# One row of wo loaded as two pieces, ahead of the third group, in a decode kernel with gated attention

## The chip, the cores and the metric

The kernel runs on one core of one Trainium2 chip. The metric is the time of one execution on the device in microseconds. Times of a kernel are given as the median of its runs. A profile is one such execution, taken by the hardware profiler; "span" is the time from its first to its last instruction, and times inside a profile count from the span's start.

## What is computed

One decode step for two sequences (B = 2, one new position each, D = 640), all in float32. Attention over a cache of 4096 positions with 32 heads of 128, a feed-forward layer with SiLU, and a gate that mixes the two:

```python
g = sigmoid((x * gate_w).sum(-1, keepdims=True))
q = (x @ wq).reshape(B, 1, 32, 128).transpose(0, 2, 1, 3)
p = softmax(einsum("bhqd,bhkd->bhqk", q, k_cache) * 128 ** -0.5)
o = einsum("bhqk,bhkd->bhqd", p, v_cache)
a = o.transpose(0, 2, 1, 3).reshape(B, 1, 4096) @ wo        # wo: 4096 x 640
b = silu(x @ w1) @ w2
return g * a + (1 - g) * b
```

The caches are by far the largest inputs; with the weights, 298 MB are read in one execution. wo is 10.5 MB of it.

## The kernel before

**Who orders the work.** The kernel first records operations, each with its engine, the names ("keys") that it reads and writes, and further operations that it comes after. Keys such as `b.3` stand for parts of a buffer. `Flow.plan` turns this into semaphore waits. Within an engine the order of recording is the order of execution, and an engine waits in place: what is queued behind a waiting operation waits too. A load is an operation of SP: SP waits for what the load depends on, issues it, and goes to the next. `f.users(keys)` gives the last writer of each key and its readers since then. An operation recorded `after` these waits for all of them, and where one of them is a load, for its landing.

**The attention.** The 32 heads of one sequence are taken four at a time (Q = 4), which makes 16 items (`items`, N = 16), ordered so that each of four groups n = 0..3 (NP = 4) has four items: two sets of four heads for each of two sequences. For an item, 8.4 MB of K and 8.4 MB of V are loaded, 64 KB to a partition. There are three such slabs in SBUF: K alternates between `a` and `b`, V goes to `v`; only the last item's V goes to `a`. In the loop over i, `products(i)` and `scores(i)` (VectorE and GpSimd) form the scores of item i, `weights(i)` the exponentials, while `values(i - 1)` multiplies V of the item before on TensorE (L799), `combine` and `gather` sum it up (L821, L837), and `turn` (L852 to L871) writes the result as columns into `oP`, the left operand of the last product. The keys of `oP` that it writes are `oP{n}{u}{b}`, one for each item, and `heads(g)` lists the four of group g.

**The output product.** wo has 4096 rows. Group g takes 1024 of them, eight for each partition (PR = 8): partition p holds rows 8p to 8p + 7 of the group side by side, 8 x 640 numbers. Groups 0, 1 and 2 lie in slab `v` after the last V there has been used, group 3 in slab `b` after the last K has been used (the last item is 15, and its K lies in `b`). `load_wo` issues them: groups 0 and 1 in one load, group 2 in one, group 3 in three cuts of 5, 2 and 1 rows (L325). Before the change all five loads are recorded together in the loop's round 15 (L909 to L912). "Row k" below is the k-th of the eight rows of every partition.

After the loop, `in_halves(g)` for g = 0, 1, 2 adds the groups' products into `early`, a PSUM tile of 128 x 320 that already holds the feed-forward's output (`ffn_out`): four strips of 32 partitions, two halves of the output's columns by two alternating places, and each strip's rows hold the two sequences 16 apart. Each row of a group is two matmuls, and each matmul in float32 shows as two instructions in the trace (L590: 64 for groups 0 and 1, 32 for group 2). `merge` copies `early` to SBUF on ScalarE (L602) and adds its strips into `acc` by a product with the matrix `join` (L607). `in_quarters(3)` then adds group 3 row by row to `acc`, four matmuls for each row (L620, eight instructions for each row, 64 in all), each row waiting for its cut. VectorE copies `acc` (L929) and SP sends out the result.

The left operand of a matmul is a window of 32 columns of `oP` (17 in `in_quarters`), which holds a group's row k for the two sequences 16 columns apart, with zeros elsewhere. `oP` has one place of 32 columns for each k and g, at LEAD + 32 * (k * NP + g), LEAD = 8.

**PSUM.** `ps_t` holds the sums of the exponentials (columns 0 and 1); `ps_acc` is `early`.

Of the kernel before, what the change touches and what calls it, by code (L numbers as in the profile page):

```python
# [189 lines left out]
def gated_decode(nc, x, kc, vc, wq, wo, w1, w2, gate, out):  # L190
    P = 128
    B, H, SK, DH = kc.shape
    D = x.shape[2]
# [13 lines left out]
    HB = 16  # L207
# [3 lines left out]
    W2 = D // 2  # L211
    NP = HQ // 2
    PR = 2 * Q
    FIRST = 5
    LEAD = HB // 2
    items = [(2 * n + u, b) for n in range(NP) for b in range(B) for u in range(2)]
    N = len(items)
    LOOPED = N - 1
# [2 lines left out]
    f = Flow(nc)  # L221
    V, S_, T_, G_ = nc.vector, nc.scalar, nc.tensor, nc.gpsimd
# [10 lines left out]
    slab = {n: slabs[:, k * SLAB : (k + 1) * SLAB] for k, n in enumerate("vba")}  # L233

    def part(n, *ks):
        return [f"{n}.{k}" for k in (ks or range(8))]

    ident = sb("ident", [P, P])
# [46 lines left out]
    PD = PR * D  # L285


    partial = slab["v"][:, (NP - 1) * PD :][:, :W2]
    ot = slab["v"][:, (NP - 1) * PD + W2 :][:, :W]

    def kslab(i):
# [22 lines left out]
    def load_wo(g):  # L314

        n, at = ("v", g * PD) if g < NP - 1 else ("b", 0)
        if g == 0:
            src = wo[: 2 * PR * P, :].rearrange("(g p n) d -> p g (n d)", g=2, n=PR)
            to = slab["v"][:, : 2 * PD].rearrange("p (g c) -> p g c", g=2)
            f.dma("SP", to, src, writes=part("v", 0, 1), after=v_users)  # L320
            return
        if g == 1:
            return
        src = wo[g * PR * P : (g + 1) * PR * P, :].rearrange("(p n) d -> p (n d)", n=PR)
        cuts = (0, PD) if g < NP - 1 else (0, FIRST * D, PD - D, PD)  # L325
        after = f.users(part(n)) if g == NP - 1 else v_users
        for k, (c0, c1) in enumerate(zip(cuts, cuts[1:])):
            f.dma("SP", slab[n][:, at + c0 : at + c1], src[:, c0:c1], writes=part(n, g % (NP - 1) + k), after=after)

    f.op("POOL", lambda: G_.memset(oP_xs, 0.0), writes=["oP", "xs"])
    f.dma("SP", slab["a"][:, : J * F], w1.rearrange("(p j) f -> p (j f)", j=J), writes=part("a"))
# [244 lines left out]
    def heads(g):  # L578
        return [f"oP{g}{u}{b}" for u in range(2) for b in range(B)]
# [32 lines left out]
        f.op("PE", fn, reads=["partial", "join"], writes=["ps_0"])  # L612

    def in_quarters(g):
        for k in range(PR):
            at = LEAD + 32 * (k * NP + g)

            def fn(k=k, at=at):
                for n in range(G):
                    last = T_.matmul(  # L620
                        acc[32 * n : 32 * n + HB + 1, :],
                        oP[:, at : at + HB + 1],
                        slab["b"][:, k * D + n * W : k * D + (n + 1) * W],
                        start=False,
                        stop=(k == PR - 1),
                    )
                return last

            f.op("PE", fn, reads=part("b", (k >= FIRST) + (k == PR - 1)) + heads(g), writes=["ps_0"])

    ffn_out("v")

# [69 lines left out]
    def products(i):  # L702
        k = slab[kslab(i)].rearrange("p (c d) -> p c d", d=DH)
        k0, k1 = part(kslab(i), 0), part(kslab(i), 1)
        f.op(
            "POOL",
            lambda: G_.tensor_mul(k[:, CV:, :], k[:, CV:, :], qsb[:, None, :].to_broadcast([P, C - CV, DH])),  # L707
            reads=["qsb"] + k1,
            writes=k1,
        )  # L710
        f.op(
            "DVE",
            lambda: V.tensor_mul(k[:, :CV, :], k[:, :CV, :], ps_q[:, None, :DH].to_broadcast([P, CV, DH])),  # L713
            reads=["ps_q"] + k0,
            writes=k0,
        )
# [170 lines left out]
    for i in range(N + 1):  # L887
        j = i - 1
        loop = j if 0 <= j < LOOPED else None

        def by(what):
            return [ops[what, j]] if loop is not None else ()

        steps.append(len(f.ops["DVE"]))
        turns.append(len(f.ops["ACT"]))
        if i < N:
            products(i)
        if j >= 0:
            values(j, by=[v_load[j]] if loop is not None else (), loop=loop)
            invert(j)  # L900
        if 1 <= i < N:
            load_v(i)
        if i < N:
            scores(i)
            if i + 2 < N:
                load_k(i + 2)
            peak(i)
            weights(i)
        if i == N - 1:  # L909
            v_users = f.users(part("v"))  # L910
            for g_ in range(NP):
                load_wo(g_)  # L912
        if j >= 0:
            combine(j)
            gather(j, by=by("combine"), loop=loop)
            turn(j)
        if i < N:
            inner = i if i < LOOPED else None
            total(i, by=[ops["exp", i]] if i < LOOPED else (), loop=inner)
            if i + 1 < N:  # L920
                query(i + 1, by=[ops["exp", i]], loop=inner)
                copy_q(i + 1)
    edges = steps[2 : N + 1 : 2]
    f.alike["DVE"] = [[f.ops["DVE"][a:b] for a, b in zip(edges, edges[1:])]]
    for g_ in range(NP - 1):
        in_halves(g_)
    merge()
    in_quarters(NP - 1)
# [60 lines left out]
```

## Time and profile before

| | |
|---|---|
| median of 3 runs | 695.91 us (695.84 to 696.04) |
| the profiled execution | 695.97 us |
| its span | 694.6 us |
| mean granted clock of TensorE | 0.661 of full speed |
| busy share of the span: DVE, POOL, PE, ACT | 73%, 38%, 31%, 6% |
| HBM read | 298.26 MB, 429 GB/s over the span |

The page has six parts: busy time of each engine; the span in 40 slices; DMA queues; the chain of work that ended last; the costliest groups of instructions; DMA issues. PE is TensorE's matmuls, PEld its weight loads, DVE VectorE, ACT ScalarE, POOL GpSimd, SP the engine that issues loads. L590 is line 590 of the kernel. A group's row gives the line, engine and operation, output and input, how often, and in brackets the time that the engine was idle just before and what ended it. In a table of stretches each row gives the busy time of PE, PEld, DVE, ACT and POOL with the number of instructions, then the granted clock of TensorE as a share of full speed, the mean busy share of the 16 DMA engines, and what they moved in GB/s. Packets are put down to the stretch in which they start, so shares over 1 occur in short stretches.

### The profile page before, as it was taken

How to read it: one execution, taken by the hardware profiler on the slowest of the kernel's cores; microseconds unless marked ns; L12 is line 12 of the kernel's file. 1: busy time of each engine (PE TensorE's matmuls, PEld its weight loads, DVE VectorE, ACT ScalarE, POOL GpSimd, SP SyncE). 2: the span in 40 equal slices, each digit the busy share in tenths (PEclk: the TensorE clock that was granted, in tenths of full speed). 3: DMA queues.
4: the chain of work that ended last, by engine and by line, in shares of the span. 5: the costliest groups of instructions: out<-in, count | busy, mean ns of one | idle time of the engine just before them, and what ended most of it. 6: DMA issues, size and time to landing. Idle time of an engine off the chain costs nothing. (4 is left out here: it accounts for less than half of the span.)

```text
span 694.6 us, 3767 instructions
## 1 busy us (share of the span) xinstructions
PE 211.9 (31%) x1440; PEld 70.2 (10%) x1440; DVE 506.9 (73%) x269; ACT 40.0 (6%) x152; POOL 265.6 (38%) x26
## 2 busy tenths in 40 slices
PE   0073033151331506060412305060513215060556
PEld 0031010010110101010100101010101001010112
DVE  3910958898989697886959596986959595977901
ACT  0001010101010101010010101010000101010100
POOL 1000908190827090815335180906244270907100
PEclk9997556565565657566575757575665757575779
DMA  9999999999999999999999999999999999999997
GB/s 383 429 426 473 426 423 427 423 464 434 423 430 423 442 457 423 423 430 434 464 423 423 430 426 468 426 423 430 423 468 430 423 430 423 453 445 423 430 417 309
DMA packets 6051, 298.32 MB, mean 429 GB/s; under 512 B 652, under 2 KB 672, under 8 KB 928
## 3 DMA queue, kind: packets, MB, share of 16 engines
q1 hardware_dynamic: 6048, 298.27, 99.3%
q8 instruction: 3, 0.05, 0.0%
HBM read 298.26 MB, written 0.01 MB: 429 GB/s over the span
## 5 line engine op out<-in xcount | busy, mean ns | idle before, releaser
L707 POOL TENSOR_TENSOR slabs<-slabs,qsb 128x7680 f32<-128x7680 f32 x16 | 262.4, 16400 | 378.9 <-DMA slabs<-in_A_k_cache_dram 330.8
L723 DVE TENSOR_REDUCE s<-slabs 128x68 f32<-128x8704 f32 (+1 forms) x32 | 276.3, 8677 | 0.0
L799 PE MATMUL ps<-slabs,pz 128*32 128x512 f32 x1024 | 147.2, 739 | 337.1 <-PEq L156 328.9
L713 DVE TENSOR_TENSOR slabs<-slabs,ps 128x8704 f32<-128x8704 f32 x16 | 147.5, 9221 | 103.8 <-DMA slabs<-in_A_k_cache_dram 103.2
L799 PEld LDWEIGHTS ps<-slabs,pz 128*32 128x32 f32 x1024 | 39.7, 132 | 433.5 <-issue 425.2
L752 ACT ACTIVATE pz<-s,nb 32x128 f32<-32x128 f32 x64 | 25.5, 398 | 545.8 <-PE ps L799 353.2
L837 PE MATMUL ps<-osb,pick 128*128 128x512 f32 x32 | 21.1, 747 | 60.9 <-PEq L156 59.9
L821 DVE SCALAR_TENSOR_TENSOR osb<-ps,rg,own 128x512 f32<-128x512 f32 x16 | 12.0, 750 | 23.4 <-PE ps L799 23.1
L852 DVE TENSOR_REDUCE row<-ps 64x128 f32<-64x512 f32 x16 | 10.9, 682 | 24.0 <-PE ps L837 24.0
L773 PE MATMUL ps<-rs,fold 128*128 128x1 f32 x32 | 6.2, 262 | 40.9 <-PEq L156 40.8
L475 DVE SCALAR_TENSOR_TENSOR slabs<-slabs 128x1728 f32<-128x1728 f32 x8 | 16.2, 2019 | 0.3
L487 PE MATMUL ps<-slabs,xz_col 128*32 128x432 f32 x16 | 3.1, 927 | 33.4 <-DVE slabs L475 33.4
L837 PEld LDWEIGHTS ps<-osb,pick 128*128 128x128 f32 x32 | 5.4, 211 | 75.0 <-issue 73.1
L752 ACT ACTIVATION_READ_ACCUMULATOR pz<-s,nb 32x1 f32 x64 | 11.8, 184 | 0.0
L773 PEld LDWEIGHTS ps<-rs,fold 128*128 128x128 f32 x32 | 6.2, 226 | 54.2 <-issue 53.3
L859 DVE STREAM_TRANSPOSE ps<-row 64x256 f32<-64x256 f32 x16 | 10.3, 643 | 0.6
L567 PE MATMUL ps<-slabs,seq 128*32 128x320 f32 x54 | 9.2, 496 | 3.7 <-DVE seq L546 3.7
L642 PE MATMUL ps<-slabs,xz_col 128*32 128x512 f32 x80 | 9.8, 593 | 0.0
L652 PE MATMUL ps<-qall,spread 128*128 (+1 forms) x32 | 9.0, 371 | 0.8 <-ACT qall L680 0.8
L929 DVE COPY slabs<-ps 128x160 f32<-128x160 f32 x1 | 0.3, 324 | 11.9 <-PE ps L620 11.9
L590 PE MATMUL ps<-slabs,oP_xs 128*32 128x320 f32 x96 | 6.9, 434 | 2.4 <-DMA slabs<-in_A_wo_dram 2.4
L652 PEld LDWEIGHTS ps<-qall,spread 128*128 128x128 f32 x32 | 6.1, 236 | 1.7 <-ACT qall L680 1.7
(63 smaller groups left out, 69.8 us busy)
## 6 DMA issues: line engine op xcount, KB each, us to landing
slabs<-in_A_wq_dram SPq DMA_DIRECT2D x1, 10240.0 KB, 44.5
slabs<-in_B_w_dram SPq DMA_DIRECT2D x2, 4320.0 KB, 16.9
slabs<-in_A_wo_dram SPq DMA_DIRECT2D x1, 5120.0 KB, 22.7
slabs<-in_A_wo_dram SPq DMA_DIRECT2D x1, 2560.0 KB, 28.3
slabs<-in_A_wo_dram SPq DMA_DIRECT2D x1, 1600.0 KB, 31.9
slabs<-in_A_wo_dram SPq DMA_DIRECT2D x1, 640.0 KB, 32.9
slabs<-in_A_wo_dram SPq DMA_DIRECT2D x1, 320.0 KB, 33.2
slabs<-in_A_k_cache_dram SPq DMA_DIRECT2D x16, 47.9
```

Source lines behind the costliest of these rows:

```text
L475: lambda b=b, j=j, at=at: V.scalar_tensor_tensor(hsum[:, b, :], w1t[:, j, :], at, hsum[:, b, :], op0=ALU.mult, op1=ALU.add)
L652: return T_.matmul(ps_q[:, :DH], spread, qall.rearrange("p n b u d -> p (n b u) d")[:, i, :], start=True, stop=True,)
L707: lambda: G_.tensor_mul(k[:, CV:, :], k[:, CV:, :], qsb[:, None, :].to_broadcast([P, C - CV, DH])),
L713: lambda: V.tensor_mul(k[:, :CV, :], k[:, :CV, :], ps_q[:, None, :DH].to_broadcast([P, CV, DH])),
L723: lambda c0=c0, c1=c1: V.reduce_sum(Ss[i % 2][:, c0:c1], k[:, c0:c1, :], axis=AX.X),
L752: last = S_.activation(pz[lo:hi, :, 4 * q : 4 * q + 4], s[lo:hi].rearrange("p (g c) -> p g c", c=4), AF.Exp, bias=nb[lo:hi], scale=SCALE, ...
L773: lambda *_: T_.matmul(ps_t[:, :1], fold.rearrange("p a q c -> p (a q c)"), rs, start=True, stop=True),
L799: last = T_.matmul(ps_v[32 * q : 32 * q + 32, :], pz[:, gr, :], v[:, gr, :], start=(gr < 4), stop=(gr >= NG - 4),)
L821: lambda: V.scalar_tensor_tensor(osb, ps_v.rearrange("p (c d) -> p c d", d=DH), rg, own[:, :, None].to_broadcast([P, 4, DH]), op0=ALU.mult ...
L837: lambda *_: T_.matmul(ps_o, pick, osb.rearrange("p c d -> p (c d)"), start=True, stop=True),
L852: lambda: V.reduce_sum(row, ps_o[:64].rearrange("p (c d) -> p d c", d=DH), axis=AX.X),
L859: lambda: V.transpose(oT.rearrange("p n (e i) -> p n e i", e=2), twice),
```

## The change

Row 7, the last of group 3's eight, no longer comes as the last cut. It is loaded ahead of group 2, in two loads: partitions 0 to 87 to their own place in slab `b` (HELD = 88), and the 40 rows of partitions 88 to 127 onto the even partitions 0, 2, ... 78 of `moved`, another place in slab `b` (MOVED = 80 partitions). The rest of group 3 comes in cuts of 5, 1 and 1 rows.

For the 40 rows, the left operand must stand on the even partitions too. `shift` is a matrix of 128 x 80 whose even columns are the columns 88 to 127 of the identity; `set_apart` multiplies `oP`'s two columns of row 7 by it on TensorE into `ps_t` and VectorE copies them to `apart`, a window like those of `oP`. `shift`, `apart` and `moved` are cleared with `blank` by one memset. `add_spared` adds both pieces into `early`, two matmuls each, before group 2; `in_quarters` has seven rows left.

What is recorded moves as well. In round 15 only groups 0 and 1 are loaded. In the round after the last item, VectorE's memset of `blank` and the copy to `shift` come first, then the two new loads, group 2 and group 3. The new loads come after all users of slab `b`, the memset among them; `load_wo(3)` asks for the users of `b` again after the new loads have been recorded. `set_apart` is recorded ahead of all of `in_halves`.

```diff
+    HELD = 8 * 11
+    MOVED = 2 * (P - HELD)
...
+    blank = slab["b"][:, PD:][:, : D + MOVED + 2 * HB + LEAD]
+    moved, shift, apart = blank[:MOVED, :D], blank[:, D : D + MOVED], blank[:MOVED, D + MOVED :]
...
-        cuts = (0, PD) if g < NP - 1 else (0, FIRST * D, PD - D, PD)
+        cuts = (0, PD) if g < NP - 1 else (0, FIRST * D, PD - 2 * D, PD - D)
...
+    def load_spared():
+        rows = wo[(NP - 1) * PR * P :, :].rearrange("(p n) d -> p n d", n=PR)[:, PR - 1, :]
+        after = f.users(part("b"))
+        f.dma("SP", slab["b"][:HELD, PD - D : PD], rows[:HELD], writes=part("b", 3), after=after)
+        f.dma("SP", moved[::2], rows[HELD:], writes=part("b", 4), after=after)
...
     def in_quarters(g):
-        for k in range(PR):
+        for k in range(PR - 1):
...
-                        stop=(k == PR - 1),
+                        stop=(k == PR - 2),
...
-            f.op("PE", fn, reads=part("b", (k >= FIRST) + (k == PR - 1)) + heads(g), writes=["ps_0"])
+            f.op("PE", fn, reads=part("b", max(0, k - FIRST + 1)) + heads(g), writes=["ps_0"])
+
+    def set_apart(g):
+        at = LEAD + 32 * ((PR - 1) * NP + g)
+        f.op(
+            "PE",
+            lambda: T_.matmul(
+                ps_t[:MOVED, 4:6], shift, oP[:, at : at + HB + 1 : HB], start=True, stop=True
+            ),
+            reads=["shift"] + heads(g),
+            writes=["ps_t"],
+        )
+        f.op(
+            "DVE",
+            lambda: V.tensor_copy(apart[:, LEAD : LEAD + HB + 1 : HB], ps_t[:MOVED, 4:6]),
+            reads=["ps_t"],
+            writes=["apart"],
+        )
+
+    def add_spared(g):
+        own_row = oP[:HELD, 32 * ((PR - 1) * NP + g) :], slab["b"][:HELD, PD - D : PD]
+        for e, (a, w) in enumerate((own_row, (apart, moved))):
+
+            def fn(e=e, a=a, w=w):
+                for n in range(2):
+                    at = LEAD // 2 * n
+                    last = T_.matmul(
+                        early[64 * e + 32 * n :][:32, :],
+                        a[:, at : at + 32],
+                        w[:, n * W2 : (n + 1) * W2],
+                        start=False,
+                        stop=False,
+                    )
+                return last
+
+            f.op("PE", fn, reads=part("b", 3 + e) + ["apart"] + heads(g), writes=["ps_acc"])
...
         if i < N:
             products(i)
+        else:
+            f.op("DVE", lambda: V.memset(blank, 0.0), writes=part("b") + ["shift", "apart"])
+            f.op(
+                "DVE",
+                lambda: V.tensor_copy(shift[:, ::2], ident[:, HELD:]),
+                reads=["ident", "shift"],
+                writes=["shift"],
+            )
+            load_spared()
+            for g_ in range(NP - 2, NP):
+                load_wo(g_)
...
             v_users = f.users(part("v"))
-            for g_ in range(NP):
+            for g_ in range(NP - 2):
                 load_wo(g_)
...
+    set_apart(NP - 1)
     for g_ in range(NP - 1):
+        if g_ == NP - 2:
+            add_spared(NP - 1)
         in_halves(g_)
     merge()
     in_quarters(NP - 1)
```

## The prediction

> **What bounds the kernel now.** I read the page first. The columns of its DMA part are queue, packets, MB and share of 16 DMA engines.
>
> ```profile
> span 694.6 us, 3767 instructions
> DMA packets 6051, 298.32 MB, mean 429 GB/s; under 512 B 652, under 2 KB 672, under 8 KB 928
> q1 hardware_dynamic: 6048, 298.27, 99.3%
> q8 instruction: 3, 0.05, 0.0%
> ```
>
> The loads keep all 16 DMA engines busy for 99.3% of the span, and the change moves not one byte less. So it can act only on what follows the moment when the first DMA engine runs out of work. The chain of waits shows that end (start, us, what):
>
> ```profile
> 657.78 31.89 DMA slabs<-in_A_wo_dram
> ...
> 689.80 2.16 PE ps L620 x56
> ...
> 691.99 0.51 PE ps L620 x8
> ...
> 692.52 0.32 DVE slabs L929
> ```
>
> The last row of wo lands, eight matmul instructions (0.51 us) and one copy follow. Third view: the last microseconds cut into stretches; the last two columns are DMA share and GB/s.
>
> ```profile
> 690.10:690.30 0.20, 0.20 (x16) 0.20 (x8) 0.00 (x0) 0.00 (x0) 0.00 (x0) 1.00 0.29 115
> 690.30:690.50 0.20, 0.20 (x13) 0.19 (x9) 0.00 (x0) 0.00 (x0) 0.00 (x0) 1.00 0.19 77
> ...
> 691.10:691.30 0.20, 0.20 (x12) 0.07 (x8) 0.00 (x0) 0.00 (x0) 0.00 (x0) 1.00 0.19 77
> 691.30:691.50 0.20, 0.20 (x12) 0.18 (x12) 0.00 (x0) 0.00 (x0) 0.00 (x0) 1.00 0.13 51
> 691.50:691.70 0.20, 0.20 (x16) 0.12 (x4) 0.00 (x0) 0.00 (x0) 0.00 (x0) 1.00 0.00 0
> ```
>
> A share of 0.19 is 3 of 16: thirteen DMA engines are done by 690.3, and three work on to about 691.4. Nobody takes work from those three, so a load's rows are tied to their DMA engine. The kernel's time is that of the slowest three, some 1.2 us behind. Three is also the number of q8 packets, which are instruction code. The DMA view of 684 to 686 us shows one of them:
>
> ```profile
> q8 instruction: 1, 0.02, 3.0%
> ```
>
> 3.0% of 16 DMA engines over 2 us is 0.96 us on one DMA engine: a DMA engine that has fetched code stays that much late to the end. That the three late ones are the three that fetched is my reading of it.
>
> **The change part by part.** *Loads.* In the rows above three DMA engines move 77 GB/s, 25.7 each, so a piece of 2560 B (one partition's row) takes 0.100 us. Taking one row out of the last cuts takes 8 pieces, 0.80 us, from every DMA engine. The 88 partitions in place give 8 pieces back to eleven of them if they are spread eight to each as the 128 are; the 40 rows give 4 pieces to ten, if four to each. So five DMA engines end 0.80 us earlier, one ends as before, ten end 0.40 us later. If the three late ones are among the five, they end at 691.4 - 0.8 = 690.6, the ten at 690.2 + 0.4 = 690.6, and the last landing moves from 691.99 to 691.2. If one of them is among the ten, it moves to 692.4.
>
> The count of small packets bears on the spread: 652 packets under 512 B are 40 x 16 + 12, a completion for each DMA engine of the forty large loads and four for each of the small loads of x, gate and the output. A load of few rows therefore does run on fewer DMA engines. [...]
>
> *SP's queue.* The two new loads wait for the memset on VectorE, and loads 2 and 3 of wo stand behind them. Load 3 also waits until the two have landed, since their keys are among those it asks for.
>
> ```profile
> 0.83 0.17 DVE L359 MEMSET ones<- 128x128 f32 x1 [0.83 <-PEq L979]
> 4.75 0.09 DVE L423 MEMSET join<- 128x34 f32 x1
> 656.84 2.31 SPq L72 DMA_DIRECT2D slabs<-in_A_wo_dram  x5
> 660.65 0.22 DVE L871 SCALAR_TENSOR_TENSOR oP_xs<-ps,side,oE 64x8 f32 x1 [0.16 <-DVE oE L865]
> 676.81 0.75 DVE L821 SCALAR_TENSOR_TENSOR osb<-ps,rg,own 128x512 f32<-128x512 f32 x1 [15.59 <-PE ps L799]
> 692.88 0.60 SPq L72 DMA_DIRECT2D out_dram<-slabs  x1
> ```
>
> The memset of 128x760 is bounded by 0.17 us and, at the 0.08 us for 94 columns between its two rows, by about 0.75; I take 0.7. It and the small copy run after 660.9, in VectorE's 15.59 us of idling. The issues slip from 657 to 662; ahead of them in the queue lie the last V, needed until 667.5, and the first 5 MB of wo until 679.6, so the slip costs nothing. The two new loads land at 679.7 to 680.9 (1.2 us behind the first groups on the ten). SP then issues three loads at 2.31 / 5 = 0.46 us each. The 8 rows of load 2 keep even a relieved DMA engine busy for 6.3 us after the first groups, to about 684. That leaves over 2 us; without this cover, each microsecond late would be one at the end.
>
> *TensorE.* The tail rows:
>
> ```profile
> 667.50 9.16 PE L799 MATMUL ps<-slabs,pz 128*32 128x512 f32 x64 [8.15 <-DMA slabs<-in_A_v_cache_dram]
> 658.96 0.38 PE L773 MATMUL ps<-rs,fold 128*128 128x1 f32 x2
> 677.61 1.12 PE L837 MATMUL ps<-osb,pick 128*128 128x512 f32 x2 [0.95 <-DVE osb L821]
> 679.63 4.51 PE L590 MATMUL ps<-slabs,oP_xs 128*32 128x320 f32 x64 [0.89 <-DMA slabs<-in_A_wo_dram]
> 680.44 0.22 DVE L871 SCALAR_TENSOR_TENSOR oP_xs<-ps,side,oE 64x8 f32<-64x8 f32 x1
> 685.64 2.36 PE L590 MATMUL ps<-slabs,oP_xs 128*32 128x320 f32 x32 [1.50 <-DMA slabs<-in_A_wo_dram]
> 688.54 0.47 PE L607 MATMUL ps<-slabs,join 128*17 128x160 f32 x8 [0.55 <-ACT slabs L602]
> 689.77 1.25 PEld L620 LDWEIGHTS ps<-slabs,oP_xs 128*17 128x17 f32 x40 [1.10 <-issue]
> 689.80 2.65 PE L620 MATMUL ps<-slabs,oP_xs 128*17 128x160 f32 x64 [0.80 <-DMA slabs<-in_A_wo_dram]
> ```
>
> `set_apart` stands first in TensorE's queue and waits for the last `turn`, which ends at 680.44 + 0.22 = 680.66. Behind it are all 64 instructions of groups 0 and 1, which now start at 679.63. They will start at 680.9 (0.05 to be released, 0.2 for the two shift instructions, half of L773's 0.38). Less about 0.43 for the last one's drain, 64 take 4.08 us, 0.065 each, so they end at 685.0; the eight of `add_spared` at 0.065 end at 685.5. Group 2 lands at 685.64, no later than now on the ten (1.2 early, 1.2 more work). So at full clock this wait is hidden.
>
> But TensorE is now idle from 678.73 to 680.7, 2.0 us instead of 0.9, and the granted clock answers to that. The windows of 3.41 us are where the clock changes; the first busy column is PE, the third from the end is the clock:
>
> ```profile
> 57.40:60.81 3.41, 1.57 (x9) 0.41 (x3) 0.00 (x0) 2.28 (x4) 0.00 (x0) 0.99 0.75 327
> 152.96:156.37 3.41, 1.85 (x20) 0.35 (x12) 3.41 (x1) 0.00 (x0) 2.73 (x1) 1.00 1.29 557
> 658.14:661.55 3.41, 1.09 (x4) 0.30 (x2) 2.07 (x6) 0.76 (x4) 0.00 (x0) 0.99 1.33 577
> 661.55:664.96 3.41, 0.00 (x0) 0.00 (x0) 0.00 (x0) 0.00 (x0) 0.00 (x0) 0.50 0.80 346
> 668.38:671.79 3.41, 3.41 (x24) 0.79 (x20) 0.00 (x0) 0.00 (x0) 0.00 (x0) 0.51 1.03 444
> 678.62:682.03 3.41, 2.52 (x37) 1.20 (x40) 1.78 (x4) 0.00 (x0) 0.00 (x0) 1.00 0.98 420
> ```
>
> After 57.40 (1.57 us busy) and 658.14 (1.09) the clock is halved; after 152.96 (1.85) and 678.62 (2.52) it is kept. A window that holds the whole 2.0 us gap is busy 1.4 us at most: halved. If a boundary cuts the gap, both windows reach 1.75 (halfway) only with the boundary between about 679.06 and 679.44, counting the 0.95 idle ahead of L837: 0.4 of 3.41 us. So in nine placements of ten one window at half clock falls on groups 0 and 1, and half of the 2.2 to 3.4 us that lies on work is lost: 1.1 to 1.7 us; I take 1.5. Group 2 then starts at 685.5 + 1.5 = 687.0. From its start to the join's is 688.54 - 685.64 = 2.90 us as now; the join's 8 issues take 0.25 (1.25 / 40 = 0.031 each), the remaining 56 of L620 1.75, the last drain 0.26 (0.51 - 0.25): 5.16 in all. The last matmul ends at 692.16, against 692.50 now. The landing at 691.2 gives 691.7, which is earlier: **TensorE ends last, 0.34 us sooner than now**.
>
> [...]
>
> **The sum.** The profiled execution took 695.97 us, 1.37 beyond its span of 694.6, and 0.06 over the median of 695.91. 695.97 - 0.34 = 695.63; against the median 695.57. I say 695.6.
>
> **The rivals.** *The clock is kept.* Then the landing decides: -0.79, 695.1. For it: one placement in ten, and a `turn` that comes earlier when the half-clock part of L799 is shorter (667.50 starts at half clock, and where the window ends is chance), so that the gap's loss is absorbed by the wait for group 2. *A late DMA engine is among the ten* that get 12 pieces and give 8: the last landing is 0.40 later, and TensorE, even halved, is hidden behind it: 696.3. No view names DMA engines. The packet records, which no view prints singly, can be joined end to start: none of the three late ones seems to be one of the four that carried x and gate, and the three begin the first load later than those four. That speaks for the five, weakly. *Slower beyond doubt:* the two new loads spread over fewer DMA engines than I took, as the small ones over four do. Four would carry 22 + 10 = 32 pieces, 3.2 us, less the 0.8 taken off. A DMA engine that is not late has 1.2 us of room, so it decides from 20 pieces on, and here it is +1.2 us; if a late one is among the four, +2.4: 697.1 to 698.3. [...] That the change does nothing, its loads shared evenly after all, is 695.9 and inside the forecast's range.
>
> **How the numbers follow.** Relieved and halved 0.45 (695.3 to 696.1 with the 1.1 to 1.7 us and the shift of `turn`); relieved, clock kept or its loss absorbed 0.18; a late one among the ten 0.27; fewer DMA engines 0.06; anything else, such as a fourth code fetch, 0.04. The first three lie within 0.2% (1.4 us, about what a measurement can tell from no change), 0.90 together. No case gains 1.4 us, 0.02 is left for the unforeseen. Slower: 0.06 + 0.02 = 0.08. The range 695.0 to 696.5 holds the first three with the bounds of their terms.
>
> **What would show it.** In the changed profile: L590's group of 64 starting at 680.7 to 681 behind `set_apart`; a granted clock of 0.5 in some window from 679 to 686 and that group lasting 5.6 to 6.2 us; no idle time of PE before the eight last matmuls. With the clock at 1.0 throughout, PE waits for a wo load there instead. After about 690.6 the DMA share should fall at once rather than stand at 0.19; a stand at 0.06 to 0.19 until 691.8 means that late ones were loaded more. A DMA share well under 0.9 between 680 and 688 would mean that SP's hold on load 3 starved the queue, which I exclude.

## The result and the profile after

| | before | changed |
|---|---|---|
| median | 695.92 us | 697.41 us |
| lowest and highest of 22 runs each | 695.66 to 697.04 | 695.93 to 698.81 |
| profiled execution, its span | 695.97, 694.6 | 696.56, 695.2 |

The ratio is 1.0021, with a 95% interval of 1.0014 to 1.0027: the change costs 1.5 us, and its runs spread over 2.9 us where the kernel before spreads over 1.4. The profiled execution of the changed kernel, at 696.56, is the fifth lowest of its 22 runs; what it shows is less than what the median pays, and the experiments have to find the rest.

The page of the changed kernel:

```profile
span 695.2 us, 3777 instructions
...
DMA packets 6200, 298.32 MB, mean 429 GB/s; under 512 B 673, under 2 KB 693, under 8 KB 1077
...
q1 hardware_dynamic: 6197, 298.27, 99.3%
q8 instruction: 3, 0.05, 0.0%
```

673 packets under 512 B are 21 more than the 652 of before, 11 + 10: the two new loads run on eleven and ten DMA engines, as the prediction took it. The bytes are the same. The chain of waits of its last part (start, us, what):

```profile
681.29 9.57 DMA slabs<-in_A_wo_dram
690.87 0.04 issue
690.91 2.14 PE ps L629 x56
693.05 0.02 issue
693.07 0.33 DVE slabs L987
```

It now ends over the landing of the cut of five rows at 690.87, behind which all 56 instructions of the last part run in one go. Before, 56 of these started at 689.80 and only the last eight waited. The last row lands at 692.40 (before 691.99), just early enough not to be waited for. So every load of the end is late, not the last one alone. TensorE's timeline (start, us, in brackets the idle time ahead and what ended it):

```profile
678.45 1.12 PE L881 MATMUL ps<-osb,pick 128*128 128x512 f32 x2 [0.95 <-DVE osb L865]
681.53 0.30 PE L644 MATMUL ps<-oP_xs,slabs 128*80 128x2 f32 x2 [1.96 <-DVE oP_xs L915]
681.77 4.51 PE L599 MATMUL ps<-slabs,oP_xs 128*32 128x320 f32 x64
...
687.12 2.36 PE L599 MATMUL ps<-slabs,oP_xs 128*32 128x320 f32 x32 [0.30 <-DMA slabs<-in_A_wo_dram]
690.02 0.47 PE L616 MATMUL ps<-slabs,join 128*17 128x160 f32 x8 [0.55 <-ACT slabs L611]
690.91 2.10 PE L629 MATMUL ps<-slabs,oP_xs 128*17 128x160 f32 x56 [0.42 <-DMA slabs<-in_A_wo_dram]
```

Groups 0 and 1 wait for `set_apart` as forecast, but run at full clock (4.51 us). Group 2 starts 1.48 us later than before (687.12 against 685.64) and ended a wait for its load: TensorE is not what is late. The stretches of the end (last two columns: DMA share, GB/s):

```profile
690.40:690.80 0.40, 0.09 (x4) 0.00 (x0) 0.00 (x0) 0.00 (x0) 0.00 (x0) 1.00 0.92 365
690.80:691.20 0.40, 0.29 (x9) 0.25 (x13) 0.00 (x0) 0.00 (x0) 0.00 (x0) 1.00 0.79 314
691.20:691.60 0.40, 0.40 (x20) 0.35 (x12) 0.00 (x0) 0.00 (x0) 0.00 (x0) 1.00 0.46 179
691.60:692.00 0.40, 0.40 (x20) 0.35 (x12) 0.00 (x0) 0.00 (x0) 0.00 (x0) 1.00 0.12 45
```

In the forecast nearly all were to be done at 690.6. Here nearly all 16 are at work until 690.8 (share 0.92) and half of them until 691.6. The bytes of 690.4 to 691.6 were missing earlier. Wider stretches of both kernels show where: first before, then changed.

```profile
666.00:674.00 8.00, 6.50 (x44) 1.68 (x48) 0.00 (x0) 0.00 (x0) 0.00 (x0) 0.64 0.98 420
674.00:682.00 8.00, 6.16 (x66) 2.01 (x62) 2.53 (x5) 0.00 (x0) 0.00 (x0) 1.00 1.01 435
682.00:690.00 8.00, 5.16 (x80) 2.07 (x76) 0.00 (x0) 0.42 (x1) 0.00 (x0) 1.00 0.97 406
```

```profile
666.00:674.00 8.00, 6.49 (x36) 1.62 (x40) 0.00 (x0) 0.00 (x0) 0.00 (x0) 0.54 1.03 443
674.00:682.00 8.00, 5.08 (x44) 1.40 (x39) 2.64 (x6) 0.00 (x0) 0.00 (x0) 1.00 0.99 369
682.00:690.00 8.00, 7.18 (x104) 3.02 (x96) 0.03 (x1) 0.43 (x1) 0.00 (x0) 1.00 0.97 412
```

From 674 to 682, while the two new loads run (they land between 678.9 and 681.3), the DMA engines are as busy as before (share 0.99) and move 369 GB/s. Measured on 420, the rate that a row of all 128 partitions in one load will have there (below), 8 x (1 - 369/420) = 0.97 us of transfer are lost. A share near one with fewer bytes says that packets take longer, not that the queue was empty. The packet records agree: row 7's pieces of 2560 B take 102 to 312 ns here, half of them 134 or more, and 102 ns each in the kernel that loads the row in one load (`whole_row`, below).

### The profile page after: what moved, and what is told of

It is laid out like the page before. It is cut to its first block, busy times and chain, and to the rows that moved or that the text cites. A ratio compares the mean times of both kernels' runs of the same rounds, so it can differ in the third digit from the quotient of the medians.

```text
span 695.2 us, 3777 instructions
## 1 busy us (share of the span) xinstructions
PE 213.5 (31%) x1442; PEld 70.7 (10%) x1442; DVE 507.4 (73%) x272; ACT 40.0 (6%) x152; POOL 265.7 (38%) x26
## 5 line engine op out<-in xcount | busy, mean ns | idle before, releaser
L843 PE MATMUL ps<-slabs,pz 128*32 128x512 f32 x1024 | 148.5, 745 | 335.4 <-PEq L156 328.1
L843 PEld LDWEIGHTS ps<-slabs,pz 128*32 128x32 f32 x1024 | 40.2, 133 | 432.4 <-issue 425.0
```

The costliest lines, as they stand in the source:

```text
L843: last = T_.matmul(ps_v[32 * q : 32 * q + 32, :], pz[:, gr, :], v[:, gr, :], start=(gr < 4), stop=(gr >= NG - 4),)
```

## The experiments

Every kernel is the changed kernel with the edit shown, unless it says otherwise. The theories, with the letters that the expectations use: **P**, TensorE's wait for the last `turn` and the half clock behind it make the time; **D**, the slow transfers from 674 to 682 make it; S and U are two causes for that slowness: **S**, a row loaded in parts, each onto fewer than 128 partitions, holds all DMA engines back while its loads run (my guess at the reason, that several DMA engines then write to the same part of the partitions, is one that no run shows); **U**, DMA engines with unequal work run apart and lose by it; **L**, which DMA engines have fetched code, and so are late, differs from execution to execution, and the changed kernel gives most of them more to do; **F**, the opposite of L, that it is the same ones each time.

**The same kernel again.** No edit.

> The changed kernel as it is, for a second profile and its spread beside the other runs. In the first profile the packets of the two new loads and those of group 2 behind them took 1.5 times their usual time between 678.2 and 681 us (280 GB/s instead of 430), which costs about 1.0 us on every DMA engine. Theory D (transfers): this stretch of 3 us is there again and decides the median of about 697.4. Theory P (TensorE's wait for the last turn, with the clock halved in most runs): the slow stretch is chance; here the clock is at 0.5 in a window between 679 and 686 and the group of 64 at in_halves takes about 6 us instead of 4.5.

Median 697.44 (695.90 to 698.94; ten runs: four up to 696.28, six from 697.13), ratio 1.0023 [1.0012, 1.0033]. Its profiled execution took 695.90 and differs from the first in both causes under dispute. Its window of 3.41 us with the gap, and the next one (third column from the end: granted clock):

```profile
677.81:681.22 3.41, 1.45 (x16) 0.63 (x18) 1.92 (x5) 0.00 (x0) 0.00 (x0) 1.00 1.07 390
681.22:684.64 3.42, 3.42 (x32) 1.31 (x25) 0.00 (x0) 0.00 (x0) 0.00 (x0) 0.50 0.97 418
```

Its chain:

```profile
680.60 6.14 PE ps L599 x64
686.74 0.54 PE ps L664 x8
687.28 2.20 PE ps L599 x32
...
690.45 1.97 PE ps L629 x56
692.42 0.02 issue
692.44 0.33 DVE slabs L987
```

This is the forecast's likeliest case in kind: 1.45 us busy, clock halved, 64 instructions in 6.2 us, no wait for a load behind them, last matmul at 692.42 where 692.16 was forecast. And it is the lowest of its ten runs, 695.90. So the half clock is real, and by itself it doesn't make the median.

**The wait moved out of the way** (`late_apart`): `set_apart` stands behind groups 0 and 1, just ahead of `add_spared`.

```diff
-    set_apart(NP - 1)
     for g_ in range(NP - 1):
         if g_ == NP - 2:
+            set_apart(NP - 1)
             add_spared(NP - 1)
```

> set_apart is recorded just ahead of add_spared, so TensorE starts groups 0 and 1 when they land and not behind the last turn; the loads are as in the change. Theory P: the median falls by 1 us or more, to 696.4 or less, and the spread of 695.9 to 698.8 shrinks to some tenths. Theory D: the median stays within 0.3 us of the changed kernel's, about 697.2, and the spread stays.

697.02 (695.89 to 699.08), ratio 1.0017 [1.0007, 1.0028]. In its profile the group of 64 starts at 680.42, waiting for its load and not for `turn`, and takes 4.51 us; the median and the spread stay. P is out as the cause of the median.

```profile
680.42 4.51 PE L599 MATMUL ps<-slabs,oP_xs 128*32 128x320 f32 x64 [1.41 <-DMA slabs<-in_A_wo_dram]
```

**40 rows on their own partitions** (`split_in_place`): no even partitions, no shift, no `set_apart`; `add_spared` is one product over all 128.

```diff
         f.dma("SP", slab["b"][:HELD, PD - D : PD], rows[:HELD], writes=part("b", 3), after=after)
-        f.dma("SP", moved[::2], rows[HELD:], writes=part("b", 4), after=after)
+        f.dma("SP", slab["b"][HELD:, PD - D : PD], rows[HELD:], writes=part("b", 4), after=after)
```

> The 40 rows go to their own partitions 88 to 127 and not onto even ones, so shift, set_apart and the second operand are gone; the two loads keep their sizes and their spread over eleven and ten DMA engines, and TensorE does not wait for the last turn. Theory P: no wait, so 695.2 to 695.6. Theory D with the uneven spread as cause: slow stretch of about 3 us at 430 to 280 GB/s as in the change, 696.5 or more. Theory D with the even partitions as cause: no slow stretch, 695.2 to 695.6.

697.57 (696.20 to 698.44), ratio 1.0021 [1.0011, 1.0030]; 369 GB/s from 674 to 682, as in the changed kernel. Where the 40 rows land doesn't matter; that the row is split in two loads is left.

**The row in one load** (`whole_row`): as `split_in_place`, with one load of 128 partitions ahead of group 2.

```diff
-        f.dma("SP", slab["b"][:HELD, PD - D : PD], rows[:HELD], writes=part("b", 3), after=after)
-        f.dma("SP", moved[::2], rows[HELD:], writes=part("b", 4), after=after)
+        f.dma("SP", slab["b"][:, PD - D : PD], rows, writes=part("b", 3, 4), after=after)
```

> Row 7 goes in one load of 128 partitions, in place, ahead of group 2: the order of the change without its uneven spread, and without shift, set_apart and a wait of TensorE. Both theories: 695.9 within 0.3, as before the change, with 2560-byte packets at 102 ns. If the slow stretch is there too, neither the uneven spread nor the even partitions cause it, but rows of 2560 bytes ahead of rows of 20480 bytes, and the time is 696.5 or more.

696.00, nine runs of ten between 695.89 and 696.27 and one at 697.46; ratio 1.0003 [0.9993, 1.0013]. Its stretch:

```profile
674.00:682.00 8.00, 5.97 (x66) 2.06 (x62) 2.52 (x5) 0.00 (x0) 0.00 (x0) 1.00 0.98 420
```

Loss and spread are both gone. The order of the loads, the memset, and the slip of the queue are all still in this kernel: the whole cost lies in the split. It relieves nobody either, so it doesn't tell S, U and L apart.

**Two halves, equal work** (`halves`): `whole_row` as two loads of 64 partitions. Each load has 16 times 4 rows, so each DMA engine gets 8 pieces, as before.

```diff
-        f.dma("SP", slab["b"][:, PD - D : PD], rows, writes=part("b", 3, 4), after=after)
+        f.dma("SP", slab["b"][: P // 2, PD - D : PD], rows[: P // 2], writes=part("b", 3), after=after)
+        f.dma("SP", slab["b"][P // 2 :, PD - D : PD], rows[P // 2 :], writes=part("b", 4), after=after)
```

> As whole_row, but row 7 comes in two loads of 64 partitions, 0 to 63 and 64 to 127. If each of the 16 DMA engines takes four rows of each load, no DMA engine gets more than another, yet the first load writes to one half of the partitions alone. Theory U (the slow stretch comes from DMA engines running apart, some already in group 2 while others have the pieces): no slow stretch, 696.0 as whole_row. Theory S (it comes from several DMA engines writing to the same few partitions' side of SBUF at once, which holds all of them back): a slow stretch from about 678.3 on, 2560-byte packets at 150 to 210 ns instead of 102, and the time longer by 0.5 to 1.5 us, 696.5 to 697.5.

697.88 (697.47 to 699.08), ratio 1.0029 [1.0018, 1.0040]. The page counts 684 packets under 512 B, 652 + 32: both loads use all 16 DMA engines, and no one is relieved or loaded more. The stretch, and then the chain:

```profile
674.00:682.00 8.00, 5.41 (x51) 1.44 (x43) 2.52 (x5) 0.00 (x0) 0.00 (x0) 1.00 1.01 338
```

```profile
682.86 9.60 DMA slabs<-in_A_wo_dram
692.46 0.04 issue
692.50 2.14 PE ps L629 x56
```

8 x (1 - 338/420) = 1.56 us are lost, and the cut of five rows lands at 692.46, 1.6 us behind the changed kernel's. U cannot make this, since the work is equal; S can. From 679 to 680 the trace shows 182 GB/s, under half of the 429 that the kernel before has over its span. Why a load of 64 partitions holds the DMA engines back is not shown, for no view tells which DMA engine writes to which partitions; that the smaller loss with 88 and 40 rows, 0.97 us, has the same cause is inferred. The runs of `halves`, with equal work for all, still spread from 697.47 to 699.08, so unequal work isn't the only source of spread.

The loss differs between executions, and the last landing goes with it. Eight profiles with the row split 88 and 40, in the order of their rate from 674 to 682, with `whole_row` and `halves` as ends (GB/s, last landing, time of the profiled execution):

| kernel | GB/s | last landing | us |
|---|---|---|---|
| whole_row | 420 | 691.79 | 695.93 |
| after_again | 392 | 691.75 | 695.90 |
| after_p4 | 392 | 691.84 | 695.99 |
| after_p5 | 389 | 691.62 | 695.81 |
| late_apart | 387 | 691.82 | 696.02 |
| after_p3 | 376 | 692.38 | 696.56 |
| changed | 369 | 692.40 | 696.56 |
| split_in_place | 369 | 692.28 | 696.43 |
| after_p2 | 364 | 692.81 | 696.97 |
| halves | 338 | 694.00 | 698.14 |

Without the loss the split rows would end at the forecast's 691.2; 392 GB/s is a loss of 0.53 us, 369 of 0.97, 364 of 1.07. With these the sum gives 691.7, 692.2 and 692.3; measured are 691.8, 692.4 and 692.8.

**Four more profiles of the changed kernel** (`after_p2` to `after_p5`), for the table and for the clock.

> The changed kernel once more, for a profile of one of its slower executions. Both theories on the slow stretch: if the time is 697 us or more, the stretch below 350 GB/s lasts longer than the 3 us of the execution at 696.56 and the 2 us of that at 695.9, by about 1.5 us for each microsecond of time. If instead the stretch is as long and TensorE waits or runs at half clock, the spread is TensorE's.

> As after_p2, one more execution: the time against the length of the stretch below 350 GB/s, and the granted clock between 679 and 686 us.

> The changed kernel, for a profile of one of its slower executions. If it takes 698 us or more: theory P, a window at half clock lies on group 2 or on the last group (32 instructions taking 4 us and not 2.4, as in own_ports), while the last landing is at 692 to 693; theory S alone, the last landing is at 694 or later.

> The changed kernel once more, for a profile of one of its slower executions. If it takes 698 us or more: theory P, a window at half clock lies on group 2 or on the last group, while the last landing is at 692 to 693; theory S alone, the last landing is at 694 or later.

A window at half clock fell on groups 0 and 1 in `after_p2` and `after_p3` (6.21 and 6.17 us for the 64), not in `after_p4` and `after_p5` (4.51). Over all six profiles it is three of six, with 696.56, 695.99 and 695.81 at full clock and 695.90, 696.97 and 696.56 at half: no order by the clock. All six lie under 697.0, though, while 22 of the 30 runs of this kernel outside these profiles lie above it, up to 698.9. None reached the 697 or 698 us for which the expectations were written, so these profiles decide nothing about the slower executions. S as they show it makes 695.8 to 697.0 and no more; something that no profiled execution of the changed kernel shows is still missing.

**Uneven work by loads of 8 rows** (`own_ports`): `whole_row`, and ten more loads of 8 rows each onto partitions four apart, whose data nothing uses, though `add_spared` waits for their landing; eight DMA engines carry 10 pieces more, a packet each (that such loads run on eight fits the landings of `tail_load`, below).

```diff
+        for n in range(10):
+            lo = 32 * (n // 4 % 2) + n % 4
+            at = PD + 2 * D + D * (n // 8)
+            f.dma("SP", slab["b"][lo : lo + 29 : 4, at : at + D], rows[lo : lo + 29 : 4], writes=[f"extra{n}"], after=after)
```

> [...] Theory U: slow stretch, 2560-byte packets over 150 ns, 696.5 or more. Theory S: no slow stretch, packets at 102 ns, 696.0 to 696.3, since the ten packets end before the three late DMA engines do, unless one of those is among the eight (then 697.0).

697.88 (696.18 to 698.71), ratio 1.0025 [1.0013, 1.0038]; 420 GB/s from 674 to 682, so none of the loss that the split row has, and yet slower, with the spread. That is neither theory's outcome: U had a slow stretch, S none and 696.0 to 696.3, or 697.0 with a late DMA engine among the eight. That S should spare loads of 8 rows on partitions four apart was part of my guess; the 420 GB/s fit it and show no reason. They also exclude the number of loads as the cause of the split row's loss, for eleven small loads stand here. Its profile is no clean witness: 1 us of extra work on eight DMA engines is in it by design, and the clock is halved at 686.64, so that group 2's 32 instructions took 3.98 us instead of 2.36. So the times spread with unequal work where transfers lose nothing, which S doesn't explain; how much of it is the clock's stays open.

**TensorE kept busy** (`warm`, then `warm2`): products that nothing uses stand in its waits, ahead of `set_apart` and behind `add_spared`. In `warm` they were of 512 columns, and the first nine took 7.9 us, 0.88 each where 0.21 was expected, so that TensorE itself became the bound.

> The changed kernel with matmuls on constants, written to a PSUM bank that nothing reads, in TensorE's two waits: nine (0.21 us each at full clock) ahead of set_apart, two ahead of group 2. They do no part of the computation. The loads are as in the change. Theory S alone (the transfers' slow stretch makes both the loss and the spread): median 697.4 and spread 695.9 to 698.9 as before. Theory S with P for the spread (the stretch costs about 0.5 us in every execution, and a window at half clock costs the slow ones 1 to 2 us more): no window at half clock after 675 us, the slowest execution below 697.3, median about 696.5.

702.49 (701.62 to 702.80): the added products were mis-sized, and it settles nothing. `warm2` has 128 columns:

```diff
+    warm(9)
     set_apart(NP - 1)
     for g_ in range(NP - 1):
         if g_ == NP - 2:
             add_spared(NP - 1)
+            warm(2)
```

> As warm, with matmuls on constants of 128 columns and not 512: two instructions of 0.11 us each, so nine take 1.9 us in the wait for the last turn and two 0.4 us ahead of group 2. In warm they took 7.9 us and TensorE ended last. Theory P for the spread: slowest execution below 697.3. Theory L or S: the spread of 695.9 to 698.9 stays, median 697.0 to 697.7, though the clock stays at 1.0 in the profile.

697.40 (695.92 to 699.12), ratio 1.0021 [1.0010, 1.0032]: as the changed kernel. TensorE's timeline, and then the stretches of the end:

```profile
678.25 2.15 PE L643 MATMUL ps<-qall,ones 128*32 128x128 f32 x18
...
680.57 4.51 PE L599 MATMUL ps<-slabs,oP_xs 128*32 128x320 f32 x64
...
687.67 2.36 PE L599 MATMUL ps<-slabs,oP_xs 128*32 128x320 f32 x32 [1.63 <-DMA slabs<-in_A_wo_dram]
```

```profile
690.80:691.20 0.40, 0.24 (x8) 0.00 (x0) 0.00 (x0) 0.00 (x0) 0.00 (x0) 1.00 0.30 115
691.20:691.60 0.40, 0.15 (x5) 0.13 (x8) 0.00 (x0) 0.00 (x0) 0.00 (x0) 1.00 0.08 32
691.60:692.00 0.40, 0.40 (x16) 0.35 (x12) 0.00 (x0) 0.00 (x0) 0.00 (x0) 1.00 0.07 26
692.00:692.40 0.40, 0.40 (x20) 0.35 (x12) 0.00 (x0) 0.00 (x0) 0.00 (x0) 1.00 0.06 26
```

The clock is full from 671 us on in this execution, and the spread of the runs is unchanged: that speaks against the clock as its cause, though the other nine were not traced. Apart from that of `warm`, this profile, at 697.16, is the only one of the row split by 88 and 40 that lies above 697.0. From 691.2 on one DMA engine of 16 works alone (share 0.06, 26 GB/s) until the last landing at 692.94; the other fifteen have landed by 691.66. The late one spent 1.0 us on a code fetch at 684.07, the third of this execution, and by the packet records joined end to start it is one of those that carry 12 pieces. That is the rival "a late DMA engine is among the ten", in one trace of a kernel with added products; `warm` shows the same, with fifteen landed by 691.75 and one at 693.21. The eight profiles of the split row without added products show the contrary: two DMA engines land well ahead of the other fourteen in each, as they would with the late three among the five relieved. So the traces show that the place differs between programs, not that it differs between executions of one.

**Added work at the end only** (`tail_load`): the kernel before, with twelve loads of 8 rows between the cut of five rows and the last two; their data is not used, but the products of the last row wait for them. Eight DMA engines carry 12 pieces more, some 1.2 us; thirteen of them have 1.2 us of room if the late three are others.

```diff
+            if (g, k) == (NP - 1, 0):
+                for m in range(12):
+                    lo, to = 32 * (m // 4 % 2) + m % 4, PD + 2 * D + D * (m // 8)
+                    f.dma(
+                        "SP",
+                        slab["b"][lo : lo + 29 : 4, to : to + D],
+                        src[lo : lo + 29 : 4, PD - D :],
...
```

> The kernel before the change with twelve loads of 8 rows (partitions four apart, as in own_ports, used nowhere) between the first and the second cut of group 3: eight DMA engines carry 12 packets more, 1.2 us, eight none. TensorE has nothing new to wait for but the last cuts. The late DMA engines end 1.2 us behind the others before the change. Theory L (which DMA engines have fetched code, and so are late, differs from execution to execution): if none of the eight is late, their 690.4 + 1.2 is no later than the late ones, 695.9 to 696.1; if one is, 1.2 us more, 697.1; both are seen, the higher one mostly. Theory F (always the same ones, not among the eight, as in the first profile of the change, where the two earliest landings are of relieved DMA engines): 695.9 to 696.1 in all executions.

Median 697.52, ratio 1.0019 [1.0009, 1.0028]. The ten runs fall in two groups with nothing between:

```
696.10 696.14 696.18 696.44 | 697.49 697.54 697.62 697.75 697.84 697.85
```

The first group is what the eight would cost with room, the second stands 1.4 us higher, about what the loads add. The profiled execution (696.14) is of the first group:

```profile
690.40:690.80 0.40, 0.40 (x21) 0.38 (x12) 0.00 (x0) 0.00 (x0) 0.00 (x0) 1.00 0.57 224
690.80:691.20 0.40, 0.32 (x12) 0.00 (x0) 0.00 (x0) 0.00 (x0) 0.00 (x0) 1.00 0.67 269
691.20:691.60 0.40, 0.24 (x8) 0.23 (x12) 0.00 (x0) 0.00 (x0) 0.00 (x0) 1.00 0.27 102
691.60:692.00 0.40, 0.40 (x16) 0.14 (x8) 0.00 (x0) 0.00 (x0) 0.00 (x0) 1.00 0.00 0
```

Five land by 690.49, and eleven, the loaded eight and the late three, from 691.49 to 692.10: eight and three, so none of the late is among the loaded. If the same three were late each time and nothing else set the second group apart, all ten runs would stand with this one. Six don't. Here are no split loads, and in the traced execution no wait of TensorE for `turn` and no change of its clock from 674 us to 690, only more work on eight DMA engines. The times fit L. They don't show it: no execution of the second group was traced.

**Relief by loads of 8 rows** (`own_relief`, then `own_relief2`): the row goes out as sixteen loads of 8 rows on partitions four apart, all by eight DMA engines, 64 rows moved, with `set_apart` just ahead of `add_spared`; the other eight are relieved of 8 pieces. `own_relief` also had the mis-sized products of `warm`.

```diff
+        for n in range(2 * 8):
+            lo, at = 32 * (n // 4 % 2) + n % 4, HELD * (n // 8)
+            to = moved if at else slab["b"][:HELD, PD - D : PD]
+            f.dma("SP", to[lo : lo + 29 : 4], rows[at + lo : at + lo + 29 : 4], writes=[f"spared{n}"], after=after)
```

> Row 7 in sixteen loads of 8 rows, each to partitions four apart, as in own_ports: partitions 0 to 63 in place, the 64 rows of partitions 64 to 127 into moved on 64 partitions; set_apart stands just ahead of add_spared, and matmuls on constants fill TensorE's waits (four and five of 0.21 us). Eight DMA engines carry 16 packets for row 7, eight carry none. Theory S: packets at 102 ns, no slow stretch; the eight end 0.86 us later than before the change, 691.0 to 691.5 for their last landings, the late ones 0.74 us sooner at 691.0 to 691.2, so the last landing is 0.4 us sooner than the 691.95 of before: 695.5, and 695.3 to 695.9 with TensorE. Theory U: slow stretch, 696.5 or more.

> [...] Packets at 102 ns, no slow stretch. Theory F with late ones only among the other eight: 695.5 to 695.9. Theory L: an execution with a late one among the eight ends at 690.5 + 0.9 + 1.2 for the landing, 696.6 to 696.9, and most executions do; group 2 comes 1.6 us later on the eight, so TensorE may add up to 1.0.

`own_relief`: 702.37 (701.99 to 703.08), bound by the added products like `warm`. `own_relief2`: 697.54, ratio 1.0036 [1.0025, 1.0047]; six runs from 697.33 to 697.57 and four from 699.07 to 700.31. Two groups once more, and 402 GB/s from 674 to 682, better than the split by 88 and 40. But its profiled execution took 697.50 with a span of 695.0: 2.5 us lie outside the span, as in `own_relief`, where the other kernels have 1.4. These two profiles alone hold a code fetch after the last instruction, 1.8 us behind it. The DMA view from 695 to 698 us:

```profile
q14 instruction: 1, 0.01, 1.1%
```

1.1% of 16 DMA engines over 3 us is 0.53 us on one, a candidate for half of the extra 1.1 us; the cause is not shown. The times are neither theory's: F had 695.5 to 695.9, L 696.6 to 696.9. In the profile five DMA engines land by 689.71 and eleven from 690.87 on, which fits the late three being among the eight relieved once more. No kernel of this study beats the one before; `whole_row` equals it.

## Why the prediction was wrong, point by point

**What bounds, and the late DMA engines: right for one execution, carried to all.** The loads bind the end, and a DMA engine that has fetched code is late to the end (`warm2`: it landed at 692.94, the others by 691.66). In the six profiles of the changed kernel the last landings of 691.6 to 692.8 fit late ones among the five relieved, as I read it from the trace of before. The sign that I gave for the rival, a DMA share standing at 0.06 to 0.19 until 691.8, came all the same (0.12 from 691.6 on): a loss shared by all makes it too. For the slower executions the runs point to a second failed step: which ones fetched is, by the times of `tail_load`, not the same in every execution, and I gave one trace's reading the weight 0.63 against 0.27. "That speaks for the five, weakly" should not have carried most of the chance. This is inferred, for no slower execution of the changed kernel was traced. With a late one among the ten, the rival's landing of 692.4 and a loss of 0.5 to 1.0 us make 692.9 to 693.4; before, 691.99 went with 695.97, so these make 696.9 to 697.4. That is where the upper six of ten runs of `after_again` begin. It isn't where they end: ten of the 22 runs lie above 697.5, up to 698.81, and what adds the rest stays open.

**Loads: counts right, price wrong.** The spread over eleven and ten DMA engines, an assumption of mine before, stands in the page (21 more small packets). That the ten are among the eleven, which makes five, one and ten, no view shows. What the runs show in its place fits it: DMA engines with 8 and then 4 pieces of 2560 B ahead of group 2 in the packet records joined end to start, and two landings ahead of the other fourteen in the eight profiles of the split row without added products. The step that the traces show to have failed is the price, "a piece of 2560 B takes 0.100 us", read off three DMA engines that had the end for themselves and applied to loads of 88 and 40 rows. While these run, transfers slow down on all DMA engines, also on those with none of the row (the two earliest end at 690.56 and 690.58, where 690.2 - 0.8 was forecast): 0.53 to 1.07 us lost, a term that the sum didn't have at all, and that no rival had. In the profiled execution it puts the last landing at 692.40 and not at 691.2. `halves` and `whole_row` show that it comes from splitting a row over part of the partitions; by what mechanism, no run shows.

**SP's queue: right.** The memset took 0.69 us against 0.7 (quoted from the list of groups, columns as on the page), it ran in VectorE's idle time, and no hole follows load 3: the DMA share is 0.97 from 682 to 690.

```profile
L943 DVE MEMSET slabs<- 128x760 f32 x1 | 0.7, 692 | 0.2 <-issue 0.2
```

**`set_apart`'s wait: right in kind.** Idle time 1.96 us against 2.0; it came at 681.5 instead of 680.9 because the half-clocked part of L843 was longer in that execution. It never set the median (`late_apart`).

**The clock: right mechanism, too sure.** The full form was seen in `after_again`. "Nine placements of ten" was three profiles of six. The changed kernel's own profile shows why it was kept there: the boundary at 680.25 cuts the gap.

```profile
676.84:680.25 3.41, 1.78 (x10) 0.30 (x2) 1.39 (x2) 0.00 (x0) 0.00 (x0) 1.00 1.10 348
680.25:683.66 3.41, 2.13 (x30) 1.15 (x34) 1.28 (x5) 0.00 (x0) 0.00 (x0) 1.00 0.98 414
```

The placement doesn't seem to be free, as I took it: in these six the windows and L843's own half-clocked part go together, and `turn` comes late in just those executions in which the boundary falls into the gap (mean clock from 666 to 674: 0.53 to 0.55 in the three that kept it, 0.65 to 0.73 in the three that lost it). 1.45 us of work in a window lost the clock, 1.78 and 2.13 kept it, on the side of the 1.75 us that I worked with, an estimate from the 1.57 that lost it and the 1.85 that kept it in the trace of before. In that trace the granted clock changes only at whole multiples of 3.413 us from one another, the windows of the prediction.

**The sum.** 695.6 was reached in kind by single executions (695.81, 695.90) and is what remains when both failed steps happen to cost little. As I read the runs, the median has both: a loss of 0.5 to 1.1 us, seen in every traced execution, and a late DMA engine with more work in about six of ten, inferred from the times. The rival that I called slower beyond doubt (fewer DMA engines than I took) gave the right time for a wrong reason: the page's 21 small packets exclude it.

## What to carry to other kernels

Where transfers bind, price a small load by its effect on all others, and prefer one load over all 128 partitions to two over parts of them, even if the count of bytes per DMA engine is the same: 128 rows in one load cost nothing here, 64 + 64 cost 2.0 us, and 88 + 40, with the unequal work that comes with them, cost 1.5. A trace is one execution: lateness with a cause that isn't tied to the data, such as a code fetch, should not be counted on to stay with the same DMA engines. Giving some of them more work then seems to make the time a matter of chance, as the two groups of runs suggest. A share of busy time near one doesn't mean full speed (0.99 went with 369 GB/s here, 0.98 with 420); read GB/s beside it.

## What the runs showed of the hardware that was not expected

- Loads of 88 + 40 rows brought all 16 DMA engines from 420 to between 364 and 392 GB/s over 8 us, loads of 64 + 64 to 338, ten loads of 8 rows on partitions four apart left them at 420 (`own_ports`), sixteen at 402 (`own_relief2`). The loads of wo under way at the same time were slowed with them: in the changed kernel their pieces of 20480 B that started from 677.66 to 680.80 took 787 to 1280 ns, the others 761 to 778.
- A code fetch of 16 KB among the loads held a DMA engine for 0.95 to 1.07 us, and nothing made that up by the end, 5 to 8 us later. It struck a DMA engine among the ten in `warm` and `warm2` and none of the ten in the eight other profiles of the row split by 88 and 40; that the place also changes between executions of one kernel is inferred from the times of `tail_load`.
- The clock of TensorE was halved after a gap of 1.96 us, with 1.45 us of work in the window of 3.41 (`after_again`; granted clock 0.50 in the next).

Open: by what mechanism the loads of a split row hold all DMA engines back, and loads of 8 rows little or not; why the loss in the split stretch varies from 0.53 to 1.07 us between executions of one kernel; what lifts the slowest runs to 698.8, beyond what the loss and a late DMA engine add up to; the 1.1 us beyond the span of `own_relief2`; how much of the spread of `own_ports` is the clock's; and the late DMA engines of an upper run, none of which was traced except that of `warm2`.
